# Moving the q and k transposes of four heads from TensorE to DMA transposes, with later output weights and a shared one-hot transpose

## The chip, the cores and the metric

The kernel runs on one core of one Trainium2 chip. The metric is device time in microseconds (us), and the kernel before takes 302.07 us, the median of three runs (301.95 to 302.08). A trace's span, from the first to the last profiled instruction, is shorter: 300.2 us here. A program on one core has no second die to compare with, so a run is called slow here only when it is over 1.5% above the fastest run of the same kernel. PE is the matrix engine (TensorE), PEld its weight loads, DVE the vector engine, ACT the scalar engine, POOL the GpSimd engine, and SP the engine that only issues DMAs here.

## The reference

Thirty-two heads (4 batches of 8) of routed attention feed one two-layer block with an exact GELU. A query may see only keys whose nearest centroid is the same.

```python
q_assign = argmax(einsum('bhsd,hcd->bhsc', q_n, c_n), -1)   # 16 centroids; the same for k
mask     = q_assign[:, :, :, None] == k_assign[:, :, None, :]
scores   = where(mask, q @ k.T / sqrt(D), -1e9)             # S = 768, D = 64
attn     = softmax(scores) @ v                              # (4, 8, 768, 64)
x        = attn.transpose(0, 2, 1, 3).reshape(3072, 512)
out      = gelu(x @ w_in) @ w_out                           # 512 -> 2048 -> 512
```

## The kernel before

The kernel is one long hand-made schedule. Each head goes through these steps.

- POOL splits q and k into a high and a low fp16 half (`st`, 384 KB for a head).
- `st` is transposed into `T`, so that the 64 dimensions lie on partitions. Heads 0 to 9 do this with 12 PE transposes and two DVE copies from PSUM. Heads 10 to 31 do it with one DMA transpose, issued on SP (`DMA_TRANSPOSE` in the traces). Crossbar transpose is only a name for it here, since no trace shows how it is done.
- PE multiplies `T` with the centroids (`asn_ps`), DVE turns the result into one-hots, the one-hots are transposed, and DVE writes them into 16 further rows of `T`. They become the mask.
- PE computes scores from `T`, ACT the exp, PE the product with v (`x_ps`).

```python
def tr_pe(i, w, ...):                      # heads 0 to 9; w = 0 for q, 1 for k
    for j in range(N):                     # N = 6
        nc.tensor.transpose(t_ps[:, j * 128:(j + 1) * 128], st[:, w, j, :], ident)
    (copy or nc.vector.tensor_copy)(Ts[i][:, w, :], t_ps)

def tr(i):                                 # heads 10 to 31
    st = sts.pop(i)
    Ts[i] = t_pool.tile([128, 2, S], FP16, tag="T", name="T")
    nc.sync.dma_start_transpose(out=Ts[i].rearrange("c w (n p) -> c (w n) p", p=128),
                                in_=st.rearrange("p w n c -> p (w n c)"))

def load_w(n):                             # 8 chunks, fp32 in memory, fp16 in SBUF
    nc.gpsimd.dma_start(out=w_chunks[n][0], in_=w_chunks[n][1])
# ... 
for n in range(1, 8):                      # chunks 0-3 are w_in, 4-7 are w_out
    at(T[n] + 0.5, load_w, n)              # one in each of heads 1 to 7
```

One chunk of weights is read as 1 MB of fp32 and written as 512 KB of fp16. From 10 to 55 us the kernel does heads 0 to 9 alone. From 55 us on, the two-layer block of a finished batch is woven between the later heads. Order is fixed by a list of times (`at`) and by a table (`PLAN`) that puts the small pieces of other heads into the six slots of each head.

The softmax here doesn't subtract the row's maximum and nothing guards it: scores larger than these inputs give would overflow.

## Time and profile before

| | before |
|---|---|
| device time | 302.07 us |
| PE busy over the span | 98% |
| share of PE in the chain that ended last | 89% |
| longest wait of PE | 0.8 us, at the start |
| heads 0 to 9 end (first load of the GELU table on ACT) | 54.95 us |

These are lines of the profile page of the kernel before. The first gives busy time of each engine. The others cut the span into 40 slices of 7.5 us: PE busy and DMA busy in tenths (9 is 90% or more), the PE clock granted in tenths, and GB/s moved.

```profile
PE 295.1 (98%) x3098; PEld 185.6 (62%) x3098; DVE 125.2 (42%) x286; ACT 214.0 (71%) x273; POOL 108.1 (36%) x183
...
PE   8899999999999999999999999999999999999996
...
PEclk9999999999999999999999999999999999999999
DMA  6999999994279258979489237866032221000122
GB/s 210 352 305 259 264 264 209 228 239 114 54 204 208 63 120 214 201 177 193 99 215 200 63 90 211 169 89 131 2 87 63 64 58 40 36 2 0 44 97 70
```

PE is full from start to end, at a granted clock of 9 tenths or more in every slice. The DMA row is full up to about 68 us, exactly where the change puts four more transfers.

The windows view gives busy time in a stretch, here from 20 to 55 us, for PE, PEld, DVE, ACT and POOL (instructions in brackets), then granted clock, DMA share and GB/s. DMA share adds up the time that packets took in all queues, so above 1, as the 1.23 here, means that packets overlapped in time. GB/s counts what is written: a weight chunk that is converted in flight counts with 512 KB, though 1 MB is read (the eight chunks are 4.19 MB in the page's software queue).

```profile
20.00:55.00 35.00, 34.42 (x559) 26.72 (x559) 28.99 (x65) 33.33 (x46) 33.52 (x52) 1.00 1.23 256
...
49.00:55.00 6.00, 5.95 (x78) 4.21 (x76) 3.24 (x7) 5.98 (x10) 5.76 (x10) 1.00 1.53 190
```

PE (34.42 of 35), ACT (33.33) and POOL (33.52) are all nearly full in this stage, and the DMA engines move 256 GB/s.

The chain that ended last (shares of the span), and the first lines of the list of PE's waits (what waited, what for, total us, times, longest):

```profile
PE 89%; DVE 6%; ACT 3%; DMA 1%; issue 0%
```

```profile
PE w_ps L98 <- PEq L654: 0.8, 1, 0.8
PE sc_ps L320 <- ACT p_sb L323: 0.4, 1, 0.4
```

No wait is for a DMA. In the timeline of SP's queue the first two transposes of `T`, of heads 10 and 11, look like this (start us, us, name):

```profile
45.09 8.63 SPq L210 DMA_TRANSPOSE T<-st  x2
```

Merely issuing the two kept SP busy for 8.63 us, and they landed 9.3 and 9.7 us after their issue. Two weight chunks were in flight with them (issued from 39.70 us on, landing after 10.2 and 12.8 us). A later transpose, issued at 73.84 us with no load and no chunk in flight and only a one-hot transpose before it (72.52 us), landed after 3.7 us.

### The profile page before, as it was taken

How to read it: one execution, taken by the hardware profiler on the slowest of the kernel's cores; microseconds unless marked ns; L12 is line 12 of the kernel's file. 1: busy time of each engine (PE TensorE's matmuls, PEld its weight loads, DVE VectorE, ACT ScalarE, POOL GpSimd, SP SyncE). 2: the span in 40 equal slices, each digit the busy share in tenths (PEclk: the TensorE clock that was granted, in tenths of full speed). 3: DMA queues.
4: the chain of work that ended last, by engine and by line, in shares of the span. 5: the costliest groups of instructions: out<-in, count | busy, mean ns of one | idle time of the engine just before them, and what ended most of it. 6: DMA issues, size and time to landing. Idle time of an engine off the chain costs nothing.

```text
span 300.2 us, 7392 instructions
## 1 busy us (share of the span) xinstructions
PE 295.1 (98%) x3098; PEld 185.6 (62%) x3098; DVE 125.2 (42%) x286; ACT 214.0 (71%) x273; POOL 108.1 (36%) x183
## 2 busy tenths in 40 slices
PE   8899999999999999999999999999999999999996
PEld 4677777666666666666566666666566565555444
DVE  5898897102664732132365732122353413000112
ACT  5699999965888888856788888865788883466000
POOL 4999999999034004574444004600000000000000
PEclk9999999999999999999999999999999999999999
DMA  6999999994279258979489237866032221000122
GB/s 210 352 305 259 264 264 209 228 239 114 54 204 208 63 120 214 201 177 193 99 215 200 63 90 211 169 89 131 2 87 63 64 58 40 36 2 0 44 97 70
DMA packets 74065, 42.85 MB, mean 143 GB/s; under 512 B 54320, under 2 KB 71088, under 8 KB 74032
## 3 DMA queue, kind: packets, MB, share of 16 engines
q1 hardware_dynamic: 69520, 38.09, 52.4%
q0 software_dynamic: 4224, 4.19, 8.4%
q8 instruction: 24, 0.39, 0.5%
q10 hardware_dynamic: 288, 0.10, 0.1%
q14 instruction: 9, 0.07, 0.1%
HBM read 27.30 MB, written 6.29 MB: 112 GB/s over the span
## 4 chain that ended last, share of the span: by engine, by line
PE 89%; DVE 6%; ACT 3%; DMA 1%; issue 0%
PE hp L395 27%; PE op L421 25%; PE sc_ps L320 18%; PE x_ps L335 10%; PE op_alt L421 3%; ACT p_sb L323 3%; PE asn_ps L228 3%; PE tr_ps L154 1%; DVE T L155 1%; DMA q_raw<-in_q_dram 1%; DVE T L276 1%; DVE T L278 1%; DVE x_tok L346 1%; PE fin_ps L359 1%; DVE asum L241 1%; DVE oh L249 0%
## 5 line engine op out<-in xcount | busy, mean ns | idle before, releaser
L323 ACT ACTIVATE p_sb<-sc_ps 128x768 f16<-128x768 f32 x192 | 148.7, 811 | 21.3 <-PE sc_ps L320 13.0
L421 PE MATMUL op<-w_out_sb,g 128*128 128x512 f16 (+1 forms) x352 | 97.1, 371 | 0.0
L320 PE MATMUL sc_ps<-T 80*128 80x384 f16 x384 | 93.7, 324 | 0.6 <-ACT p_sb L323 0.4
L395 PE MATMUL hp<-xt,w_in_sb 128*128 128x384 f16 x504 | 85.0, 326 | 0.0
L400 ACT ACTIVATE g<-hp 128x768 f16<-128x768 f32 x63 | 51.1, 811 | 37.2 <-PE hp L395 37.1
L335 PEld LDWEIGHTS <-p_sb 128*128 128x128 f16 x1152 | 53.7, 97 | 29.8 <-DVE x_tok L346 0.6
L395 PEld LDWEIGHTS <-w_in_sb 128*128 128x128 f16 x504 | 47.9, 98 | 30.4
L335 PE MATMUL x_ps<-vaug,p_sb 128*128 128x65 f16 x1152 | 58.5, 193 | 0.0
L421 PEld LDWEIGHTS <-g 128*128 128x128 f16 x416 | 38.9, 97 | 30.2
L132 POOL CAST st<-q_raw 128x384 f16<-128x384 f32 x30 | 15.6, 520 | 77.3 <-DMA q_raw<-in_q_dram 56.0
L425 DVE COPY o_sb<-op 128x512 f32<-128x512 f32 (+1 forms) x22 | 14.8, 672 | 55.0 <-PE op L421 54.9
L241 DVE TENSOR_REDUCE asum<-asn_ps 128x192 f32<-128x384 f32 x30 | 16.7, 557 | 50.4 <-PE asn_ps L228 50.3
L320 PEld LDWEIGHTS <-T 80*128 80x128 f16 x384 | 26.5, 97 | 4.7 <-DVE T L278 0.5
L135 POOL TENSOR_TENSOR st<-k_raw,st 128x384 f16<-128x384 f32 x30 | 27.4, 913 | 2.4
L133 POOL TENSOR_TENSOR st<-q_raw,st 128x384 f16<-128x384 f32 x30 | 27.4, 912 | 2.5
L345 DVE RECIPROCAL rec<-x_ps 128x6 f32<-128x6 f32 x32 | 6.2, 193 | 42.4 <-PE x_ps L335 42.4
L228 PEld LDWEIGHTS <-T 128*128 128x128 f16 x360 | 15.6, 96 | 5.5 <-DVE T L155 0.8
L228 PE MATMUL asn_ps<-c_all,T 128*128 128x32 f16 x360 | 18.0, 177 | 0.4 <-DVE T L155 0.2
L346 DVE TENSOR_TENSOR x_tok<-x_ps,rec 128x384 f16<-128x384 f32 x32 | 17.8, 558 | 1.1
L143 POOL CAST vaug<-v_raw 128x384 f16<-128x384 f32 x32 | 16.1, 508 | 0.0
L134 POOL CAST st<-k_raw 128x384 f16<-128x384 f32 x30 | 15.3, 510 | 0.0
L284 DVE TENSOR_SCALAR T<-ohT 16x768 f16<-16x768 f16 x22 | 9.4, 428 | 6.9 <-DMA ohT<-oh 6.4
(73 smaller groups left out, 144.6 us busy)
## 6 DMA issues: line engine op xcount, KB each, us to landing
q_raw<-in_q_dram SPq DMA_DIRECT2D x32, 192.0 KB, 4.0
k_raw<-in_k_dram SPq DMA_DIRECT2D x32, 192.0 KB, 4.1
v_raw<-in_v_dram SPq DMA_DIRECT2D x32, 192.0 KB, 4.2
out_dram<-o_sb SPq DMA_DIRECT2D x23, 256.0 KB, 2.3
w_in_sb<-in_moe_w_in_dram POOLq DMA_DIRECT2D x4, 512.0 KB, 9.8
w_out_sb<-in_moe_w_out_dram POOLq DMA_DIRECT2D x4, 512.0 KB, 10.4
T<-st SPq DMA_TRANSPOSE x22, 4.7
ohT<-oh SPq DMA_TRANSPOSE x11, 2.8
```

The costliest lines, as they stand in the source:

```text
L133: nc.gpsimd.tensor_sub(st[:, 0, :, D:2 * D], q_raw, st[:, 0, :, 0:D])
L135: keng.tensor_sub(st[:, 1, :, D:2 * D], k_raw, st[:, 1, :, 0:D])
L143: nc.gpsimd.tensor_copy(va[:, :, 0:D], vraws.pop(i))
L228: nc.tensor.matmul(a_ps[:, j, which], t[:, js], c_all[:, :, chs], start=True, stop=True)
L241: nc.vector.tensor_reduce(out=asum, in_=a_ps.rearrange("p n w l c -> p n w c l"), axis=AX.X, op=ALU.add)
L320: nc.tensor.matmul(s_ps[:, t, 0:QB], Ts[i][0:D + C, 1, c * 128:(c + 1) * 128], Ts[i][0:D + C, 0, t * QB:(t + 1) * QB], start=True, stop=True)
L323: nc.scalar.activation(ps[i][:, c, :].rearrange("p (t q) -> p t q", t=2), s_ps[:, :, 0:QB], ACT_FN.Exp, bias=0.0, scale=float(scale))
L335: nc.tensor.matmul(x_ps[:, j], ps[i][:, ch, j * 128:(j + 1) * 128], va[:, ch, 0:D + 1], start=(ch == 0), stop=(ch == N - 1))
L346: nc.vector.tensor_tensor(xtoks[i - i % 2][:, :, i % 2, :], x_ps[:, :, 0:D], rec.to_broadcast([128, N, D]), op=ALU.mult)
L395: nc.tensor.matmul(hp[:, t, 0:QB], w_in_sb[:, m, f * 128:(f + 1) * 128], xts[b][:, m, t * QB:(t + 1) * QB], start=(m == 0), stop=(m == NM ...
L400: nc.scalar.activation(g.rearrange("p (t q) -> p t q", t=2), hp[:, :, 0:QB], ACT_FN.Gelu, bias=0.0, scale=1.0)
L421: nc.tensor.matmul(op[:, 0:w], gs[b][f][:, js], w_out_sb[:, f, ms], start=(f == 0), stop=(f == NF - 1))
```

## The change

Its intent is to take work from the full PE. Heads 6 to 9 are transposed by DMA as well, so 48 PE transposes and eight DVE copies go. The four chunks of output weights are not needed before about 74 us, so they are issued later, with the splits of heads 10 to 13, to be out of the way of the new transposes. The one-hots of heads 8 and 9 are transposed together, which saves six more PE transposes. `PLAN` is rearranged to suit. The diff, cut to its core:

```diff
+    def pair_pe(i):
+        ohtr_pe(i)
+        aug(i)
 ...
     PT = 10
+    DT = 6
 ...
-        (4, 0): ((5, 'oneh'), (2, 'norm'), (6, 'trq'),),
+        (4, 0): ((5, 'oneh'), (2, 'norm'),),
 ...
-        (5, 0): ((6, 'oneh'), (3, 'norm'), (7, 'trq'),),
-        (5, 1): ((6, 'onep'),),
+        (5, 0): ((3, 'norm'), (6, 'asq'), (6, 'ask'), (6, 'oneh'),),
+        (5, 1): ((4, 'av0'), (4, 'av1'),),
 ...
-        (7, 1): ((8, 'onep'),),
+        (7, 1): ((9, 'asq'), (9, 'ask'), (9, 'oneh'),),
-        (7, 3): ((9, 'trk'), (9, 'asq'),),
+        (7, 3): ((8, 'onep2'),),
 ...
-        (8, 1): ((9, 'onep'),),
+        (8, 1): (),
 ...
-    for n in range(1, 8):
+    for n in range(1, 4):
         at(T[n] + 0.5, load_w, n)
 ...
+        if 10 <= h <= 13:
+            at(sp_t + 0.05, load_w, h - 6)
+        if DT <= h < PT:
+            at(sp_t + 3.5, tr, h)
```

(`asq`, `ask` are the assignment matmuls of q and k, `oneh` the one-hots, `onep` and `onep2` their transpose for one head or a pair, `trq`, `trk` the PE transposes, `av` the product with v.)

More of the change, by code (lines that the diff above doesn't have):

```diff
@@ L515 @@
         (3, 5): ((2, 'av4'), (2, 'av5'),),
-        (4, 0): ((5, 'oneh'), (2, 'norm'), (6, 'trq'),),
+        (4, 0): ((5, 'oneh'), (2, 'norm'),),
         (4, 1): ((5, 'onep'),),
         (4, 2): ((3, 'av0'), (3, 'av1'),),
-        (4, 3): ((6, 'trk'), (6, 'asq'),),
-        (4, 4): ((3, 'av2'), (3, 'av3'), (6, 'ask'),),
-        (4, 5): ((3, 'av4'), (3, 'av5'),),
-        (5, 0): ((6, 'oneh'), (3, 'norm'), (7, 'trq'),),
-        (5, 1): ((6, 'onep'),),
-        (5, 2): ((4, 'av0'), (4, 'av1'), (7, 'asq'),),
-        (5, 3): ((7, 'trk'), (4, 'av2'),),
-        (5, 4): ((2, 'fin'), (7, 'ask'),),
-        (5, 5): ((4, 'av3'), (4, 'av4'), (4, 'av5'),),
-        (6, 0): ((7, 'oneh'), (4, 'norm'), (8, 'trq'),),
+        (4, 3): ((3, 'av2'),),
+        (4, 4): ((3, 'av3'), (3, 'av4'),),
+        (4, 5): ((3, 'av5'),),
+        (5, 0): ((3, 'norm'), (6, 'asq'), (6, 'ask'), (6, 'oneh'),),
+        (5, 1): ((4, 'av0'), (4, 'av1'),),
+        (5, 2): ((6, 'onep'),),
+        (5, 3): ((4, 'av2'), (4, 'av3'),),
+        (5, 4): ((2, 'fin'), (7, 'asq'), (7, 'ask'),),
+        (5, 5): ((4, 'av4'), (4, 'av5'),),
+        (6, 0): ((7, 'oneh'), (4, 'norm'),),
         (6, 1): ((7, 'onep'),),
         (6, 2): ((5, 'av0'), (5, 'av1'),),
-        (6, 3): ((8, 'trk'), (5, 'av2'),),
-        (6, 4): ((5, 'av3'), (8, 'asq'), (8, 'ask'),),
-        (6, 5): ((8, 'oneh'), (5, 'av4'), (5, 'av5'), (5, 'norm'),),
-        (7, 0): ((9, 'trq'),),
-        (7, 1): ((8, 'onep'),),
+        (6, 3): ((5, 'av2'),),
+        (6, 4): ((5, 'av3'), (8, 'asq'), (8, 'ask'), (8, 'oneh'),),
+        (6, 5): ((5, 'av4'), (5, 'av5'), (5, 'norm'),),
+        (7, 0): (),
+        (7, 1): ((9, 'asq'), (9, 'ask'), (9, 'oneh'),),
         (7, 2): ((6, 'av0'), (6, 'av1'),),
-        (7, 3): ((9, 'trk'), (9, 'asq'),),
-        (7, 4): ((6, 'av2'), (6, 'av3'), (9, 'ask'),),
-        (7, 5): ((6, 'av4'), (9, 'oneh'), (6, 'av5'),),
+        (7, 3): ((8, 'onep2'),),
+        (7, 4): ((6, 'av2'), (6, 'av3'),),
+        (7, 5): ((6, 'av4'), (6, 'av5'),),
         (8, 0): ((6, 'norm'), (4, 'fin'),),
-        (8, 1): ((9, 'onep'),),
+        (8, 1): (),
         (8, 2): ((7, 'av0'), (7, 'av1'),),
@@ L608 @@
               "asq": lambda h: asn(h, 0, h not in ONE), "ask": lambda h: asn(h, 1, h not in ONE),
-              "oneh": lambda h: onehot(h, h not in ONE), "onep": one_pe,
+              "oneh": lambda h: onehot(h, h not in ONE), "onep": one_pe, "onep2": pair_pe,
               "fin": lambda h: fin(h, pe=True), "norm": norm,
```

## The prediction

> **What bounds the kernel now.** The page gives PE 98% of the 300.2 us span, ACT 71%, and PE is the engine of 89% of the chain that ended last. The timeline splits this. From about 55 us on, PE runs matmuls back to back (fc1, fc2, scores) and never waits. From 10 to 55 us (heads 0 to 9) three engines are nearly full: in the windows from 20 to 50 us PE is 98%, ACT 94%, DVE 89% and POOL 96% busy. In the PE timeline one head there takes 4.82 us (scores start at 25.36 and 30.18), and its matmul work is 4.7 us. Six exps run back to back in 4.33 to 4.46 us; ACT then idles 0.2 to 0.35 us per head, waiting for PE scores.
>
> **Removed.** Per head of 6 to 9: 12 PE transposes at 0.055 us (six take 0.33 us) = 0.67 us of PE, and two DVE copies at 0.56 us = 1.1 us. Sharing one transpose of the one-hots saves six more (0.33 us). PE: 54 transposes, 3.0 us; DVE: eight copies, 4.5 us. They lie in the slots of heads 4 to 7 (8 for the one-hots), which are on the chain.
>
> **What that is worth.** PE falls to about 4.0 us per head, DVE to 3.3, so ACT's six exps (4.35 us) become the limit. Heads 4 to 7 last from 28.56 to 47.64 = 19.08 us; at ACT's pace 17.4. At most 1.7 us is gained, less than the 3.0 us of PE removed. Later stages are PE-bound with unchanged work and pass the gain on.
>
> **Added.** Four DMA transposes, 384 KB each, in a stage where the DMA row already shows 9 everywhere (20 to 50 us). The same transposes later land 3.7 us after issue when alone, 4.2 to 5.4 us beside loads, but 9.3 and 9.7 us at 45 to 57 us, where two weight chunks were in flight; the second also held the SP queue for 6.2 us. [...] Moving the four output chunks (issued at 31 to 40 us) behind splits 10 to 13 (estimate: 41 to 54 us) clears most of that, but input chunks issued at 23.2 and 27.3 us land only at 33 and 37.
>
> **Critical path.** The transpose of head 6 can issue when its split ends, 26.95 us. It is wanted at the start of head 5, about 32.7 us: 5.8 us of room. I expect 6 to 9 us, so a PE stall of 0 to 3 us, about 0.7 us of it hidden by the scores ahead of ACT. Head 7 follows through the same SP queue and is wanted 2.9 us later; head 9 may meet the first output chunk. Expected stalls: 1 to 2 us in all, giving back most of the gain. The output weights should land by 65 us, fc2 wants them at 74: harmless. Pool order of splits stays.
>
> **Prediction.** 301.6 us, 299.8 to 305.0. Faster by over 2%: 0.01; within 2%: 0.95; slower by over 2%: 0.04.
>
> **Signs.** Right: T copies (DVE) for heads 6 to 9 gone; DVE under 80% from 30 to 50 us; first GELU table load at 53.2 to 55 us (54.95 before); waits of PE weight loads or assignment matmuls for the DMA of T appear near 33 and 36 us; T landings there 6 to 9 us; after that stage each interval as before. If there is no such wait, the time is about 300.4.
>
> **What would make it wrong.** Transposes pacing the whole stage (landings over 9 us for all four) would cost 3 to 5 us; late transposes of heads 10 and 11 beside the moved weights could stall PE around 64 us.

302.07 us, less at most 1.7 us of gain, plus 1 to 2 us of stalls, came to 301.6 us.

## The result, and the profile after

The change takes 314.32 us, the median of four runs (316.55, 309.61, 312.24 and 316.40), beside 302.01 us for the kernel before on the same chip. The ratio is 1.0294, with a 95% interval of 1.0249 to 1.0338. Ratios here are the mean time of one kernel's fast runs over that of the other's fast runs in the same rounds, so they are not quite the ratios of the medians quoted. The change is slower by about 3%.

The profiled run is the 316.55 one, which counts as slow by its distance from 309.61. So sizes read from it belong to that run, and a run of 309.61 must have lost less. An experiment below (the change without the shared one-hot transpose) ran at 316.2 to 317.6 in all four runs, is fast by its own measure, and shows the same two waits.

The page of the changed kernel, the same lines (slices are 7.9 us):

```profile
PE 297.0 (94%) x3044; PEld 184.7 (59%) x3044; DVE 120.4 (38%) x278; ACT 213.8 (68%) x273; POOL 108.5 (34%) x183
...
PE   8999394799999999999999999999999999999995
...
PEclk9999879699999999999999999999999999999999
DMA  7999999999535953799848834891512403000022
GB/s 237 327 300 206 143 236 213 246 218 255 123 75 141 235 79 89 217 205 170 192 107 211 169 75 113 217 178 29 100 33 52 85 35 92 35 0 2 34 99 70
```

PE has two holes, in slices 5 and 7, and the clock sags after each (8 and 7 tenths in slices 5 and 6, 6 in slice 8). There are 54 fewer PE instructions, as planned, yet PE is busy 1.9 us longer, because the clock was lower for a while (0.55 and 0.51 in the windows below). In slice 5 (31.5 to 39.4 us) the DMA row is full while only 143 GB/s are moved, where the kernel before moved 264 in its own fifth slice.

The chain that ended last, and the first of PE's waits:

```profile
PE 79%; DMA 10%; POOL 6%; ACT 2%; SPq 1%; DVE 1%; issue 1%; POOLq 0%
```

```profile
PE asn_ps L228 <- DMA T<-st: 11.3, 2, 6.2
```

A tenth of the chain is now DMA, and PE waits twice, 11.3 us in all, for a `T` to land. PE's timeline shows where (start us, us, what; in square brackets the idle time before and what ended it):

```profile
33.31 0.49 PE L324 MATMUL sc_ps<-T 80*128 80x384 f16 x2
38.92 0.51 PE L228 MATMUL asn_ps<-c_all,T 128*128 128x32 f16 x12 [5.12 <-DMA T<-st]
39.26 0.80 PE L324 MATMUL sc_ps<-T 80*128 80x384 f16 x2
...
56.86 0.50 PE L228 MATMUL asn_ps<-c_all,T 128*128 128x32 f16 x12 [6.18 <-DMA T<-st]
```

The first wait is for head 6, the second for head 9. A pair of score matmuls takes 0.49 us before the first wait and 0.80 us after it. In the first wait PE runs nothing else (0.00 of 5.10 us, in the windows below): the next scores, which follow the assignment matmuls of the late head in the program, come only after them, at 39.26 us, and ACT starves (busy 0.91 of the 5.10 us).

SP's timeline shows when the transposes were issued, heads 6, 7, 8, 9, and then 10 with 11:

```profile
27.27 2.24 SPq L210 DMA_TRANSPOSE T<-st  x1
31.96 6.66 SPq L210 DMA_TRANSPOSE T<-st  x1
40.47 1.55 SPq L210 DMA_TRANSPOSE T<-st  x1
45.30 1.29 SPq L210 DMA_TRANSPOSE T<-st  x1
51.84 15.18 SPq L210 DMA_TRANSPOSE T<-st  x2
```

Landing took 11.6, 10.3, 6.2 and 11.5 us for heads 6 to 9, and 15.9 and 9.7 for heads 10 and 11. Lines of the DMA view, at the issue of head 6 and of head 9 (the last figure is us from issue to landing):

```profile
T<-st SPq DMA_TRANSPOSE x1, 11.6
...
T<-st SPq DMA_TRANSPOSE x1, 11.5
```

The issue of head 7 held the queue for 6.66 us, until 38.62 us, while head 6's transpose was in flight until 38.87; and the loads of q, k and v between the transposes fill the rest of it: from 27.3 to 46.6 us SP has no gap over 0.2 us. So head 9 is issued at 45.30, though its split was done by 38.02 by POOL's timeline. (The chain names POOL for the time between the two landings; POOL's last whole split before 45.30 had ended at 41.86, so I take the queue's order as the main cause. SP's own list of waits puts 6.5 us of head 7's issue down to POOL too, but head 7's split was done by 31.4, before that issue began. It also puts down 1.4 us of a load just before head 9's transpose, at 43.58, and these may be a true wait.)

The windows view around the two waits (columns as before):

```profile
33.80:38.90 5.10, 0.00 (x0) 0.00 (x0) 0.30 (x1) 0.91 (x2) 4.50 (x7) 0.82 1.48 171
38.90:44.46 5.56, 5.54 (x69) 4.18 (x70) 2.48 (x6) 2.91 (x4) 5.29 (x8) 0.55 1.30 265
50.67:56.86 6.19, 0.01 (x2) 0.01 (x1) 0.37 (x1) 0.93 (x2) 4.54 (x7) 0.78 1.28 174
56.86:61.01 4.15, 4.15 (x48) 3.12 (x49) 2.29 (x5) 2.01 (x3) 3.19 (x5) 0.51 1.17 270
61.01:68.65 7.64, 7.32 (x99) 5.14 (x97) 3.73 (x9) 7.53 (x11) 0.76 (x3) 1.00 1.25 217
```

After each wait PE is full again, but at a granted clock of 0.55 for 5.6 us and 0.51 for 4.2 us. The kernel before, with no wait over 0.8 us, never lost its clock (9 tenths or more in every slice). Shorter waits than these were followed by slow matmuls too: in e4 below, after 2.62 us of waiting (to 87.54 us) pairs of score matmuls took 0.80 and 0.83 us at 88.48 and 90.32 us, and 0.51 again at 91.72. In e3, after 2.20 us (to 39.66 us), they kept 0.48 to 0.49 us, at a clock of 1.00 from 38 to 43 us. Why the clock falls, and after how long a wait, these runs do not settle.

**Where the time went.** The first GELU table load moves from 54.95 to 68.84 us, 13.9 us later, and the span grows by 14.6 us. Nearly all is lost in this stage, the two-layer block just starts later. I compare head 9's way with that in an experiment below whose transposes are on time (e4_w_clear): issued 7.2 us later (45.30 for 38.08), landing 5.6 us slower (11.5 for 5.9), and 1.0 us more from head 9's first matmul after the landing to the first long run of the two-layer block (11.79 for 10.76), with the clock low. The sum is 13.9 us (68.65 for 54.79).

### The profile page after: what moved, and what is told of

Same layout as the page of the kernel before. It is cut to its first block, busy times and chain, and to the rows that moved or that the text cites. A ratio compares the mean times of both kernels' runs of the same rounds, so it can differ in the third digit from the quotient of the medians.

```text
span 314.8 us, 7292 instructions
## 1 busy us (share of the span) xinstructions
PE 297.0 (94%) x3044; PEld 184.7 (59%) x3044; DVE 120.4 (38%) x278; ACT 213.8 (68%) x273; POOL 108.5 (34%) x183
## 2 busy tenths in 40 slices
DMA packets 80337, 44.42 MB, mean 141 GB/s; under 512 B 60592, under 2 KB 77360, under 8 KB 80304
## 3 DMA queue, kind: packets, MB, share of 16 engines
q1 hardware_dynamic: 75792, 39.66, 54.5%
q0 software_dynamic: 4224, 4.19, 9.0%
## 4 chain that ended last, share of the span: by engine, by line
PE 79%; DMA 10%; POOL 6%; ACT 2%; SPq 1%; DVE 1%; issue 1%; POOLq 0%
PE hp L399 26%; PE op L425 23%; PE sc_ps L324 15%; PE x_ps L339 9%; DMA T<-st 7%; PE op_alt L425 3%; PE asn_ps L228 2%; POOL st L133 2%; ACT p_sb L327 2%; POOL st L135 2%; DMA q_raw<-in_q_dram 2%; POOL st L132 1%; DMA v_raw<-in_v_dram 1%; POOL st L134 1%; SPq L74 1%; POOL vaug L143 1%
## 5 line engine op out<-in xcount | busy, mean ns | idle before, releaser
L324 PE MATMUL sc_ps<-T 80*128 80x384 f16 x384 | 96.0, 331 | 1.6 <-ACT p_sb L327 1.3
L339 PEld LDWEIGHTS <-p_sb 128*128 128x128 f16 x1152 | 55.2, 99 | 31.1 <-issue 1.2
L339 PE MATMUL x_ps<-vaug,p_sb 128*128 128x65 f16 x1152 | 59.9, 195 | 0.0
L425 PEld LDWEIGHTS <-g 128*128 128x128 f16 x416 | 38.9, 97 | 30.2
L429 DVE COPY o_sb<-op 128x512 f32<-128x512 f32 (+1 forms) x22 | 14.8, 672 | 55.2 <-PE op L425 52.7
L228 PE MATMUL asn_ps<-c_all,T 128*128 128x32 f16 x360 | 17.5, 177 | 11.8 <-DMA T<-st 11.3
L135 POOL TENSOR_TENSOR st<-k_raw,st 128x384 f16<-128x384 f32 x30 | 27.3, 911 | 2.4
L133 POOL TENSOR_TENSOR st<-q_raw,st 128x384 f16<-128x384 f32 x30 | 27.3, 910 | 2.5
```

The source lines that it names most:

```text
L133: nc.gpsimd.tensor_sub(st[:, 0, :, D:2 * D], q_raw, st[:, 0, :, 0:D])
L135: keng.tensor_sub(st[:, 1, :, D:2 * D], k_raw, st[:, 1, :, 0:D])
L228: nc.tensor.matmul(a_ps[:, j, which], t[:, js], c_all[:, :, chs], start=True, stop=True)
L324: nc.tensor.matmul(s_ps[:, t, 0:QB], Ts[i][0:D + C, 1, c * 128:(c + 1) * 128], Ts[i][0:D + C, 0, t * QB:(t + 1) * QB], start=True, stop=True)
L339: nc.tensor.matmul(x_ps[:, j], ps[i][:, ch, j * 128:(j + 1) * 128], va[:, ch, 0:D + 1], start=(ch == 0), stop=(ch == N - 1))
L425: nc.tensor.matmul(op[:, 0:w], gs[b][f][:, js], w_out_sb[:, f, ms], start=(f == 0), stop=(f == NF - 1))
```

## The experiments

My theory was: the new transposes land late because weight chunks and loads use the same DMA engines (the page counts the packets of both queues on 16 engines, 54.5% and 9.0% of their span in the change), PE stalls behind them as in the first wait above, and the SP queue passes the lateness on (head 9 issued at 45.30 us, its split done by 38.02). The rivals were: (B) the moved output chunks do the harm; (C) a DMA transpose is slow in itself, whatever else runs; (D) the lower clock (0.55 and 0.51) is the main loss; (E) the new order of pieces, or the shared one-hot transpose, is bad; and later (F) it is the conversion of the weights in flight. Times alone could not tell these apart, since a loss healed in one place often came back in another, so each trace was read too. All ran in rounds beside the kernel before, which stayed at 301.8 to 302.4 us each time.

| run | device us, median (range) | ratio | result right |
|---|---|---|---|
| e1_w_early | 320.24 (319.15–324.11) | 1.0642 | yes |
| e2_w_late_only | 302.56 (302.00–303.86) | 1.0020 | yes |
| e3_plain_copy | 307.99 (302.46–310.38) | 1.0072 | no |
| e4_w_clear | 312.46 (311.23–317.15) | 1.0328 | yes |
| e5_warm_fill | 318.74 (312.61–320.41) | none given | yes |
| e6_two_heads | 312.67 (309.12–313.81) | 1.0325 | yes |
| e7_free | 308.44 (305.08–313.39) | 1.0111 | no |
| e8_w_first | 316.70 (316.09–317.26) | 1.0483 | yes |
| e9_two_heads_b | 311.82 (308.82–312.66) | 1.0306 | yes |
| e10_no_pair | 316.95 (316.24–317.59) | 1.0491 | yes |
| e11_pair_only | 304.21 (303.94–304.31) | 1.0067 | yes |
| e12_no_cast | 307.42 (307.16–307.43) | 1.0178 | no |
| e13_cast_half | 307.12 (307.11–307.42) | 1.0171 | no |
| e14_change_no_cast | 313.19 (312.13–319.63) | 1.0364 | no |
| e15_spread | 302.37 (301.60–304.75) | 1.0028 | yes |

### e1_w_early: the change with the output chunks at their old places

```diff
-    for n in range(1, 4):
+    for n in range(1, 8):
         at(T[n] + 0.5, load_w, n)
-        if 10 <= h <= 13:
-            at(sp_t + 0.05, load_w, h - 6)
```

> Change kept, but all weight chunks loaded at their old places (output chunks issued at 31 to 40 us again). Theory A (the crossbar transposes of heads 6 to 9 lose to weight chunks on the shared DMA engines, and PE waits for them): the head 6 transpose is unchanged (lands near 38.8 us, PE stall about 5 us), those of heads 7 and 8 now meet output chunks and land later than the 10.3 and 6.2 us they took, so 310 to 318 us, no better than the change as given. Rival B (moving the output weights into the transposes of heads 9 to 11 is what hurt): the second stall (6.2 us before head 9's assignment) disappears and the time falls to about 306 us.

It took 320.24 us, above the 310 to 318 that I expected. Head 6 landed after 11.4 us, head 7 after 21.2 us, and the issues of heads 7 and 8 held SP for 9.60 and 9.25 us. PE's waits, beside the 11.3, 2, 6.2 of the change:

```profile
PE asn_ps L228 <- DMA T<-st: 14.4, 2, 9.4
```

So moving the output chunks helped the change. Rival B falls for this stage.

### e2_w_late_only: the kernel before, with only the output chunks moved

```diff
-    for n in range(1, 8):
+    for n in range(1, 4):
         at(T[n] + 0.5, load_w, n)
+        if 10 <= h <= 13:
+            at(sp_t + 0.05, load_w, h - 6)
```

> Kernel before, with only the four output chunks moved four heads later. Theory A: no PE wait, 302.0 us within 0.5 us, although the transposes of heads 10 and 11 land later than 9.7 us. Rival B: the move itself costs, 305 us or more.

It took 302.56 us, the same as before. The transposes of heads 10 to 12 landed after 8.3, 12.0 and 14.8 us (head 10 sooner than I expected), and PE waited for none: they were down at 50.4, 57.3 and 68.2 us, and PE takes up the first assignments after 55 us at 65.2 us. Moved alone, the chunks cost nothing that these rounds can show. So the harm needs both, the chunks and the extra transposes.

### e3_plain_copy: plain DMA copies of the same bytes for heads 6 to 9

The result is wrong, since nothing is transposed.

```diff
+    def tr_copy(i):
+        st = sts.pop(i)
+        Ts[i] = t_pool.tile([128, 2, S], FP16, tag="T", name="T")
+        nc.sync.dma_start(out=Ts[i].rearrange("c w s -> c (w s)"),
+                          in_=st.rearrange("p w n c -> p (w n c)"))
-            at(sp_t + 3.5, tr, h)          # heads 6 to 9
+            at(sp_t + 3.5, tr_copy, h)
```

> Wrong result on purpose: the four DMA transposes of heads 6 to 9 become plain DMA copies of the same 384 KB between the same tiles, with the same waits and the same place in the SP queue. If the crossbar transpose itself (its many small packets) is what is slow beside weight chunks: the copies land in 7 us or less after issue, the stalls shrink to under 1 us each, PE keeps full clock, total 300 to 302 us; this is then also the value of the PE work taken away. If bytes or the SP queue are what is short (rival C): landings stay near 10 us and the total stays above 308 us.

The copies landed after 6.4, 8.2, 7.4 and 4.9 us in place of 11.6, 10.3, 6.2 and 11.5, and the two long waits shrank to one of 2.2 us for head 7. My bound of 7 us was missed by two of the four. The time was not the 300 to 302 us that I expected in all runs: 302.46 and 306.13 us in the two fast ones. In the profiled run, a slow one, heads 10 and 11, still by DMA transpose beside the output chunks, landed after about 20 us (19.3 and 20.8), and PE waited 2.8 us for late one-hots there. The windows view from 27 to 39 us, of the kernel before, of the change, and of this run:

```profile
27.00:39.00 12.00, 11.85 (x211) 9.49 (x209) 10.62 (x25) 11.28 (x16) 11.50 (x18) 1.00 1.17 263
```

```profile
27.00:39.00 12.00, 6.61 (x106) 4.62 (x104) 5.21 (x12) 7.48 (x11) 11.05 (x19) 0.92 1.37 148
```

```profile
27.00:39.00 12.00, 9.81 (x159) 6.95 (x156) 8.12 (x18) 10.37 (x15) 11.43 (x20) 1.00 1.07 263
```

The same bytes move at 263 GB/s as copies. With the transposes the DMA engines are busier (1.37 for 1.07) and move 148 GB/s. Part of this is that SP, held by the issue of head 7, asks for fewer loads; but with what was asked, packets were in flight all the time (share 1.37) and landed late (10.3 us for head 7). The two kernels differ in their packets: by the page's counts a transpose of `T` is 1,568 packets, (80,337 − 74,065) / 4, of about 250 B, and a copy is 144. So it is not only that there is more to move: with transposes in place of copies beside the weight chunks, less was moved in the same time (148 GB/s for 263). Rival C is half right: the transpose is slower than a copy here (11.6 us for 6.4 in head 6), but the one at 73.84 us of the kernel before, beside no load and no chunk, landed in 3.7 us.

### e4_w_clear: no weight chunk from 2 to 7 issued before head 11's split

```diff
-        if 10 <= h <= 13:
-            at(sp_t + 0.05, load_w, h - 6)
+        for n in {11: (2,), 12: (3,), 13: (4,), 14: (5,), 15: (6, 7)}.get(h, ()):
+            at(sp_t + 0.05, load_w, n)
```

> Change kept, but input chunks 2 and 3 and all output chunks are loaded only with the splits of heads 11 to 15, so that no weight chunk is in flight while the transposes of heads 6 to 8 are. Theory A: those transposes land 4 to 6 us after issue, the stall before head 6's assignment falls below 1 us, the clock stays full, total 300 to 303 us. Rival C (SP queue order or the loads of q, k and v are what delays them): landings stay above 8 us and the total stays above 306 us.

The stage was healed. Heads 6 to 9 landed after 5.0, 4.4, 7.1 and 5.9 us, no wait in it was over 0.41 us, and the table load came at 54.98 us. From the first exp of head 4 to that point took 26.10 us (26.39 before). But the loss only moved. The chunks now met the transposes of heads 10 to 12, which landed after 10.4, 19.6 and 19.4 us, and PE waited 2.6 us for late one-hots and, in its timeline:

```profile
78.47 0.50 PE L228 MATMUL asn_ps<-c_all,T 128*128 128x32 f16 x12 [3.41 <-DMA T<-st]
```

The whole took 312.46 us, so the 300 to 303 us that I expected were missed. Moved back in this dense form, the chunks just met other transposes.

### e5_warm_fill: idle PE time filled with matmuls that nobody reads

```diff
+            for _ in range({6: 22, 9: 26}.get(i, 0)):     # at the assignments of heads 6 and 9
+                nc.tensor.matmul(asns[i][:, 0:512], ones[:, 0:128], ones[:, 0:512], ...)
```

> Change kept, with 22 and 26 dummy 128x512 matmuls (about 0.21 us each) put on PE just before the assignment matmuls of heads 6 and 9, where PE stood idle for 5.1 and 6.2 us. If part of the loss is the PE clock that falls after an idle stretch (granted 0.55 and 0.51 in the 5.6 and 4.1 us after the two stalls): the clock stays at 1.00 there, score slots keep 0.70 us instead of 1.28, and the total falls by 3 to 4 us to 306 to 311 us. If the lower clock costs nothing, the total stays at 310 to 316 us.

(Six matmuls of this shape take 1.29 us in the kernel before, from 75.49 to 76.78 us; here the first 22 took 4.98 us.) My expectation was missed: 318.74 us, three of four runs slow, so no ratio. The trace has a clock of 1.00 after the first wait, yet head 9 was issued at 45.43 us, as in the change, and PE just waited longer for it. So after the first wait the slow clock was hidden in the second wait. The second filling ran out 3.1 us too early, and there the clock fell anyway (0.60 from 59 to 63 us). Rival D is not the main loss; the experiment could not size the second slow stretch.

### e6_two_heads, e9_two_heads_b: DMA transposes for heads 8 and 9 only

Both start from the kernel before, without the shared one-hot transpose. The first loads the chunks 3 to 7 at the splits of heads 10 to 14. The second has all input chunks issued by 24 us and output chunks at the splits of heads 10 to 13.

```diff
-        (6, 0): ((7, 'oneh'), (4, 'norm'), (8, 'trq'),),
+        (6, 0): ((7, 'oneh'), (4, 'norm'),),               # and likewise the other rows of 8, 9
+    DT = 8
+        if DT <= h < PT:
+            at(sp_t + 3.5, tr, h)
```

> Kernel before, but only heads 8 and 9 transposed by DMA (one-hots as before), input chunk 3 and the output chunks loaded with the splits of heads 10 to 14. Theory A with room enough: both transposes land within 6 us of issue, before PE wants them (about 41 and 45 us); no stall; the gain is 0 to 0.7 us: 301.3 to 302.3 us. If DMA time as such is short in the first 75 us, later transposes (heads 10 to 13) or one-hots come late and the total is above 302.5 us.

> As the run with only heads 8 and 9 by DMA, but all input chunks issued by 24 us and only the four output chunks left for heads 10 to 13 (as in the run that moved them alone, which had no wait). If transposes and weight chunks must only be kept apart: heads 8 and 9 land in under 7 us, the GELU table load comes at 54.2 to 54.4 us instead of 54.95, no PE wait for a transpose, 301.3 to 301.8 us. If the transposes of heads 10 to 12 still come late (over 20 us, as in that run), PE waits near 70 us and the total is above 305 us.

In the stage both did what the change was meant to do: heads 8 and 9 landed after 4.8 to 6.1 us, with no wait, and the table load came at 54.24 and 54.20 us, 0.7 us earlier than before. Then heads 10 and 11 landed beside the output chunks after 20.8 and 22.1 us in e6 and 22.3 and 15.5 us in e9 (20.3 and 19.1 in a second trace of e9, with a span of 309.9 us for 307.0), and the totals were 312.67 and 311.82 us. PE's waits in e9:

```profile
PE sc_ps L320 <- DVE T L287: 3.8, 1, 3.8
PE asn_ps L228 <- DMA T<-st: 1.5, 1, 1.5
```

The first of these is for the one-hots of heads 10 and 11. Their transpose goes through SP too, and was issued only at 79.5 us, behind the transposes of `T`.

### e7_free: the change with a constant T for heads 6 to 9

The result is wrong. It asks what the removed PE and DVE work is worth when nothing takes its place.

```diff
-            at(sp_t + 3.5, tr, h)          # heads 6 to 9
+            at(sp_t + 3.5, Ts.__setitem__, h, Tfree[h - DT])
```

> Wrong result on purpose: the change's schedule, but heads 6 to 9 use constant tiles filled at the start, so there is neither a PE nor a DMA transpose for them. The stretch from the first exp of head 4 to the first GELU table load is 26.4 us before. If the work taken off PE and DVE is worth what I predicted (1.7 us), it falls to 24.7 us; if ACT's own pace and the one-hot chain limit (as the run with weights cleared suggests, 26.1 us), it falls by 0.3 to 1 us only. The total is shifted by the filling at the start and is not compared.

From the first exp of head 4 to the table load took 25.64 us, 0.75 us less than before (26.39); I had expected 1.7 us. That is the whole prize in the stage. (By a count of six exps for each head, the exp that I start from, at 28.56 us in the kernel before, is the last of head 3. It is the same one in every run, so the differences stand.) The rest of the run is not comparable, as its start was late and heads 10 and 11 still met the chunks (one wait of 4.6 us for late one-hots).

### e8_w_first: all weight chunks issued at the very start

```diff
+    for dst, src in w_chunks:              # before everything else on POOL's queue
+        nc.gpsimd.dma_start(out=dst, in_=src)
```

> Change kept, all eight weight chunks issued before anything else. The start is delayed by 5 to 20 us; what counts is the time from the first exp to the end, 290.2 us in the kernel before. Theory A (weight chunks beside transposes are the cause): no weight chunk is in flight in the stage, transposes of heads 6 to 11 land in 4 to 7 us, no PE wait over 1 us, 289 to 291 us from first exp to end. If loads of q, k, v and the SP queue are enough to delay them, PE waits over 2 us remain and it is above 293 us.

Missed: 316.70 us. I had thought that they would be through by 25 us; the last one landed at 44.1 us, and head 6 was not issued before 38.29 us and landed after 8.1, with a wait of 6.9 us. But then no chunk was left, and heads 7 to 11 landed after 4.3 to 6.0 us, and PE waited no more than another 0.3 us for a `T`.

### e10_no_pair and e11_pair_only: the shared one-hot transpose

The first is the change without the sharing; the second is the kernel before with it, where head 9's assignments have to come earlier.

```diff
# e10, against the change                     # e11, against the kernel before
-        (7, 3): ((8, 'onep2'),),             -        (7, 1): ((8, 'onep'),),
+        (7, 3): ((8, 'onep'),),              +        (7, 1): ((9, 'trk'), (9, 'asq'),),
-        (8, 1): (),                          ...      (7, 4): ((8, 'onep2'), ...),
+        (8, 1): ((9, 'onep'),),              +        (8, 1): (),
```

> The change with its one-hot pair undone (heads 8 and 9 each transpose their one-hots, as before). The pair is worth 6 transposes (0.33 us of PE) and is not on the path that the stalls set: the stalls before the assignments of heads 6 and 9 stay (5 and 6 us), the total stays at 309 to 317 us. If the pair is to blame for the second stall, the total falls below 306 us.

> Kernel before with the one-hot pair of heads 8 and 9 alone (transposes on PE, head 9 prepared four slots earlier): 0.33 us less PE work where ACT is nearly full: 301.7 to 302.5 us.

In e10 the same two waits stand, in four runs that agree within 0.5% and are all fast:

```profile
39.25 0.50 PE L228 MATMUL asn_ps<-c_all,T 128*128 128x32 f16 x12 [5.48 <-DMA T<-st]
...
56.58 0.51 PE L228 MATMUL asn_ps<-c_all,T 128*128 128x32 f16 x12 [6.33 <-DMA T<-st]
```

A second trace of e10, of a shorter execution (span 312.3 us for 315.1), has the same two waits at 3.8 and 3.2 us. The pairing did not make the loss, so this half of rival E falls. e11 was a miss: I expected 301.7 to 302.5 us and it took 304.21 (1.0067, interval 1.0055 to 1.0079). In its DVE timeline four writes of one-hot rows come in a row from 48.44 to 50.7 us, and the next head's `rec` waits behind them:

```profile
50.16 0.56 DVE L291 TENSOR_SCALAR T<-oh_ps 16x768 f16<-16x768 f16 x1
50.75 0.20 DVE L349 RECIPROCAL rec<-x_ps 128x6 f32<-128x6 f32 x1
```

It saves 0.33 us of PE (six transposes) and costs 2 us in this placement. In the change, where DVE has fewer copies, that need not be so; the change without the pair was not faster.

### e12_no_cast and e13_cast_half: half the weights read, without and with conversion

Both are e9 with output chunks of half the columns. e12 writes them as fp32 to a scratch (512 KB read, 512 KB written); e13 converts them (512 KB read, 256 KB written). The expectation of e12 says that the number of rows stays; that was a slip, its packets are longer and fewer (2,688 in the software queue for 4,224, with the same 4.19 MB).

```diff
# e12
-        w_chunks[4 + f] = (w_out_sb[:, 4 * f:4 * f + 4], w_out_r[:, 4 * f:4 * f + 4])
+        w_chunks[4 + f] = (scr[f % 3], w_out_r[:, 4 * f:4 * f + 4, 0:DM // 2])
# e13
+        w_chunks[4 + f] = (w_out_sb[:, 4 * f:4 * f + 4, 0:DM // 2],
+                           w_out_r[:, 4 * f:4 * f + 4, 0:DM // 2])
```

> Wrong result on purpose. As the second run with heads 8 and 9 by DMA, in which the transposes of heads 10 and 11 landed 22.3 and 18.9 us after issue beside the output chunks, but each output chunk is now a load of the same 512 KB without change of type (half as many float32 values, into a scratch tile, same queue, same number of 1 KB rows written; the output weights are a constant filled at the start, which shifts the whole kernel). If the conversion in flight is what collapses the DMA rate beside transposes: they land in under 10 us, no PE wait for them, and from first exp to end it takes 290 us or less (297.1 in that run, 290.2 in the kernel before). If any such chunk of that queue does it: still 15 us or more, with PE waits or late one-hots, above 293 us.

> Wrong result on purpose (the other half of the output weights is a constant filled at the start, which shifts the kernel). As the second run with heads 8 and 9 by DMA, but each output chunk loads and converts only half of its columns: 512 KB read, as in the run without conversion, and 256 KB written. If conversion with its many small packets is the cause: the transposes of heads 10 and 11 land 13 us or more after issue and PE waits or late one-hots return (above 291 us from first exp to end). If bytes are the cause: they land as in the run without conversion (9.0 and 12.4 us) or sooner, with no PE wait, 290 us or less.

Both start about 5 us late, since a memset that they need delays POOL at the start. So I count from the first exp to the end: 289.9 and 289.8 us, where the kernel before has 290.2 and e9 297.1. Heads 10 and 11 landed after 11.6 and 13.1 us in e12, so the 10 us that I expected were missed, and after 10.0 and 8.4 in e13 (22.3 and 15.5 in e9), and PE waited for none of them. (The 18.9, 9.0 and 12.4 us in my expectations were misread: each is a median of two transposes. Read rightly, e12's landings lie between its two branches; its waits and its time are those of the first.) The windows from 49 to 55 us of e9, and from 55 to 61 of e12, whose first exp is 5.6 us later:

```profile
49.00:55.00 6.00, 5.95 (x75) 4.07 (x72) 2.49 (x6) 5.98 (x9) 5.82 (x10) 1.00 1.58 110
```

```profile
55.00:61.00 6.00, 5.95 (x65) 3.97 (x64) 2.09 (x5) 5.98 (x8) 5.75 (x10) 1.00 1.09 185
```

In e9 the DMA engines are busier than in any other window shown here (1.58) and move 110 GB/s; with half the weights they are less busy (1.09) and move 185. But e9's chunks read twice what they count here, so these rates do not measure the healing; the landings do. After e12 alone one might have blamed the conversion; e13 converts, has as many software DMA packets in all as e9 (4,224), and heals as well. So conversion alone does not do it, and rival F falls. What the two share is that half as much is read in a chunk (512 KB for 1 MB).

### e14_change_no_cast: the change itself, with chunks 1 to 7 halved

```diff
+    for n in range(1, 8):
+        w_chunks[n] = (scr[n % 3], w_in_r[:, :, n * DQ:n * DQ + DQ // 2] if n < 4
+                       else w_out_r[:, 4 * n - 16:4 * n - 12, 0:DM // 2])
```

> Wrong result on purpose. The change as given, but chunks 1 to 7 are loads without change of type of half as many values into scratch tiles, at the same places in the same queue (weights are constants filled at the start, which shifts the kernel). If conversion is the cause: the transposes of heads 6 to 9 land in under 9 us, PE waits for them for less than 2 us in all (11.3 us in the change), and first exp to end takes 289 to 292 us (290.2 before, 304.5 in the change). If any chunk does it: waits above 5 us remain and it is above 295 us.

It starts 11 us late for the same reason. Its transposes landed after 6.7, 5.2, 5.9 and 4.9 us (11.6, 10.3, 6.2 and 11.5 in the change), and no wait for a transpose is left among PE's (the first line is the late start):

```profile
PE tr_ps L161 <- DVE cent_norm L188: 10.3, 1, 10.3
PE sc_ps L331 <- ACT p_sb L334: 1.3, 5, 0.4
```

From the first exp to the end it took 289.8 us (before 290.2, change 304.5). This shows that the order of pieces in the change is sound, so the rest of rival E falls, and that even with transposes on time it would be worth only 0.4 us in all.

### e15_spread: e9 with the output chunks as eight halves, spread

This one computes the right result. The halves go at the splits of heads 6, 7 and 10 to 15, with the same bytes in all.

```diff
-    w_chunks += [(w_out_sb[:, 4 * f:4 * f + 4], w_out_r[:, 4 * f:4 * f + 4])
-                 for f in range(4)]
+    w_chunks += [(w_out_sb[:, 2 * f:2 * f + 2], w_out_r[:, 2 * f:2 * f + 2])
+                 for f in range(8)]
+        if h in (6, 7) or 10 <= h <= 15:
+            at(sp_t + 0.05, load_w, h - 2 if h < 10 else h - 4)
```

> Right result. The second run with heads 8 and 9 by DMA, with the four output chunks cut into eight halves, two of them issued with heads 6 and 7 and one each with heads 10 to 15. If the rate of weight traffic is the cause: transposes of heads 8 to 12 land in under 12 us (22.3 and 18.9 us for heads 10 and 11 at the full rate), no PE wait for them, GELU table load near 54.2 us, 301.3 to 302.0 us. If not: 20 us again and above 305 us.

It took 302.37 us, ratio 1.0028 (0.9997 to 1.0059), against 1.0306 for e9. Heads 8 to 13 landed after 5.6, 4.7, 7.0, 7.1, 10.8 and 12.6 us, and in its list of waits no transpose appears:

```profile
PE w_ps L98 <- PEq L659: 0.8, 1, 0.8
PE sc_ps L320 <- ACT p_sb L323: 0.6, 2, 0.4
```

```profile
49.00:55.00 6.00, 5.95 (x74) 4.12 (x73) 2.87 (x6) 5.98 (x9) 5.75 (x10) 1.00 1.22 219
```

From 49 to 55 us it moves 219 GB/s at a DMA share of 1.22, where e9 moved 110 at 1.58. The stage ends 0.7 us sooner (44.26 us from first exp to table load, 44.98 before), but the later part gives it back: 290.3 us from first exp to end. It ties with the kernel before and does not beat it, and none of my variants does.

### What the experiments settle

Shown: the loss comes from DMA transposes that are in flight together with weight chunks at a high rate (e1 was worse with more chunks beside them, 21.2 us for head 7; heads 6 to 9 were healed in e4 without chunks, at 4.4 to 7.1 us, and in e14 with half as much read, at 4.9 to 6.7; e8 was healed once the chunks were through, at 4.3 to 6.0; and in the version for two heads e15 healed e9 with the same bytes at a lower rate, 7.0 and 7.1 us for heads 10 and 11 in place of 22.3 and 15.5). Shown: the issue behind a late transpose also held the SP queue (6.66 us for head 7 in the change), which made the next ones late (head 9 issued at 45.30 us for 38.08 in e4). The slowing is mutual: the chunks too, which take about 10 us before (medians 9.8 and 10.4), landed after up to 15.5 us in e9. By the pages a packet of a transpose has about 250 B (384 KB in 1,568), and one of a chunk about 1 KB (4.19 MB in 4,224).

Open: why the total rate falls, to 148 GB/s in the change and 110 in e9. That the small packets of the transposes do it is a guess that nothing here isolates. Open too is why heads 10 to 12 took 8 to 15 us in e2 and up to 22 us in e9 beside chunks issued in the same way, though e9 has two more transposes before them. Lastly, the run-to-run spread of the change (309.6 to 316.6 us) has no trace of a fast run behind it.

## Why the prediction was right or wrong

The prediction was 301.6 us with a range of 299.8 to 305.0; the result is 314.32 us, outside it, in a class that was given 4%.

- **Right: what bounds the kernel, and the place.** The stage to 55 us is the one that matters, and later stages only shift (13.9 of 14.6 us were lost by the table load). `T` copies went, PE lost 54 instructions, waits of the assignment matmuls for `T` appeared, the first between 33.8 and 38.9 us. The fear was named too: "Transposes pacing the whole stage (landings over 9 us for all four) would cost 3 to 5 us". Three of four were over 9 us, and even that cost was too small: the stage lost 13.9 us.
- **Wrong, the step that failed: "I expect 6 to 9 us, so a PE stall of 0 to 3 us", and "Expected stalls: 1 to 2 us in all".** Landing took 11.6, 10.3, 6.2 and 11.5 us, and the stalls were 5.1 and 6.2 us, 11.3 in all. I had landings of 9.3 and 9.7 us beside two chunks in the trace before, and still took 6 to 9 us for head 6, though its neighbours in flight were two input chunks as well.
- **Wrong: "Moving the four output chunks … clears most of that".** It does help (e1 against the change), but the input chunks at 23.5 and 27.6 us still met heads 6 and 7. Through the queue behind head 7's 6.66 us issue, head 9 was issued at 45.30 us (38.08 in e4), in the middle of the output chunks issued at 42.3 and 46.4 us. The prediction saw both pieces ("Head 7 follows through the same SP queue", "head 9 may meet the first output chunk") and did not add them up.
- **Missing: the clock.** After the two long waits PE ran at a granted clock of 0.55 and 0.51 for 5.6 and 4.2 us. The first slow stretch was absorbed in the next wait (e5), the second cost about 1.0 us by comparison of traces.
- **Over-sized: "At most 1.7 us is gained".** The removed work is worth 0.75 us in the stage (e7), and 0.4 us over the whole run (e14). ACT, which had only 0.2 to 0.35 us of idle per head to give, became the limit (busy 17.46 of 18.17 us for the 24 exps from 32.55 us in e7), and two of the short idles that it kept come with waits of PE for one-hots (0.3 us each).
- **Right: the output weights are harmless for the second layer**, and alone for the whole (e2, 1.0020). The risk for heads 10 and 11 beside moved weights was named; in the change their landing (15.9 and 9.7 us) caused no further wait on PE, in e4, e6 and e9 it did.

## What to carry to other kernels

Cost a DMA transpose with the landing time that it has next to the traffic it will really meet, not with its time alone (11.6 us for head 6 here, for 3.7 alone), and add the time that its issue holds the queue (6.66 us for head 7), because one late transfer made the next ones late (head 9 issued 7.2 us later). When a stage's DMA row is already full, look at GB/s as well as at busy: full rows with falling GB/s (148 and 110 here, for about 260) were here the sign that transfers hurt each other, and spreading a bulk load in smaller pieces over a longer time healed it in e15 (219 GB/s) without touching the transposes. And before taking work from an engine at 98%, check how near the others are: here 3.0 us less PE work was worth 0.75 us at best.
